# Sigmoid attention and an MLP-mixer block on one core: work by single batch in place of batch pairs, with every engine's order from a list scheduler

## The chip, the core and the metric

The kernel runs on one core of a Trainium2 chip (trn2). The metric is the device time of one execution in microseconds (us), as the median of several runs. Lower is better. Before the change it was 425.11 us, the median of three runs (424.64 to 426.28).

The engines are called as the profile calls them. PE is the TensorE (matmuls; PEld is its loading of weights), DVE the VectorE, ACT the ScalarE, POOL the GpSimd and SP the SyncE, which only issues DMA here. "PEclk" is the clock that the TensorE was granted. A profile covers one execution, and its "span" is about 1.9 us shorter than the time measured for the same execution.

## The reference

The inputs are fp32: 8 batches, 12 heads, 448 rows and 64 columns per head. The attention has no softmax. Each head's score goes through a sigmoid by itself, and the result feeds a mixer block that mixes first over rows (tokens), then over columns (channels).

```python
# cut to what matters
scores = (1/sqrt(64)) * (q @ k.T) - log(448)          # per batch and head: 448 x 448
attn   = sigmoid(scores)
x      = (attn @ v) as [8, 448, 768]                  # the 12 heads side by side

h  = relu(x.T @ w_tok1) @ w_tok2                      # 448 -> 256 -> 448, over rows
u  = x + h.T
h2 = relu(u @ w_ch1) @ w_ch2                          # 768 -> 1536 -> 768, over columns
out = u + h2
```

## The kernel before

The row number is split as `s = 7 p + j`, so a row block `j` has 64 rows. The kernel takes **two batches at a time**. Partitions 0 to 63 hold 64 rows of one batch, and partitions 64 to 127 those of the other. Six pairs of heads make up the attention of one batch pair. All matmuls are fp16.

```python
def load(g, i, what):              # g: batch pair, i: head pair
    ...                            # v: cast to fp16 by the DMA, on the gpsimd queue
    t = pa.tile([128, 2, J, E], FP32, tag="raw", ...)        # k and q: loaded as fp32 (sync queue)
    ...
    eng = nc.vector if (g, i) == (0, 0) else nc.gpsimd       # and cast by an engine
    eng.tensor_copy(out=t, in_=raw.rearrange("p h j e -> p j h e"))

def turn(i):                       # k and q with the head's column on the partitions
    if g > 0:  nc.sync.dma_start_transpose(...)              # by DMA
    else:      ... nc.tensor.transpose(...)                  # the first pair: on PE

def scores(i, j):                  # 64x64 tiles of the PE array, four matmuls side by side
    for b in range(2):
        for h in range(2):
            nc.tensor.matmul(out=ps[64*b:64*b+64, h, 0:S], lhsT=kT[i][64*h:64*h+64, j, b, :],
                             rhs=qT[i][64*h:64*h+64, :, b, :], ...)
    nc.scalar.activation(out=at, in_=ps, func=SIGMOID, bias=bias_t, scale=att_scale)

def values(i):                     # 28 matmuls on 64x64 tiles
    ...
    for b in range(2):             # then two copies on ACT
        nc.scalar.activation(out=xt[:, :, b, :], in_=ps[b]..., func=COPYF)

def back(i):  ...                  # 7 PE transposes: x with rows on the partitions
# tok1, tok2, uturn: the token stage; uturn turns u back on PE (6 transposes for each j)

def ch1(cb, j0, j1):               # j0..j1 is 0..4 or 4..7: 512 or 384 columns
    for db in range(NDB):          # 6 matmuls
        nc.tensor.matmul(out=ps, lhsT=w_ch1_t[:, db, 128*cb:128*cb+128], rhs=uT[:, db, j0:j1, :], ...)
    nc.vector.tensor_scalar(...)                             # relu

def ch2(j, half):                  # 12 matmuls of 384 columns, then add and store
    ...

def weave(att, mix):               # scores of pair g+1 spread among the mixer work of pair g
    ...

with tc.manual_schedule(engines={mybir.EngineType.PE}):      # only PE's order is given
    for _, _, f in attention_atoms(0):                       # the whole attention of pair 0 first
        f()
    for g in range(NG):
        front, rest = mixer_atoms(g)
        ...                                                  # tok1, loads of pair g+1
        weave(attention_atoms(g + 1), rest)
```

The mixer of pair 0 cannot start until all the attention of two batches is done. Only PE's order is fixed by the author; the other engines' orders are left to the framework.

Of the kernel before, what the change touches and what calls it, by code (L numbers as in the profile page):

```python
# [17 lines left out]

@with_exitstack
def kernel(  # L20
# [12 lines left out]

    nc = tc.nc
# [7 lines left out]
    NG = B // 2  # L42
    NP = H // 2
# [3 lines left out]
    JA = 4  # L47
    att_scale = 1.0 / math.sqrt(E)
    att_bias = -math.log(S)

    assert (B, H, S, E) == (8, 12, 448, 64) and D == 768 and TT == 256 and CC == 1536

    pc = ctx.enter_context(tc.tile_pool(name="pc", bufs=1))
    pa = ctx.enter_context(tc.tile_pool(name="pa", bufs=2))
    pp = ctx.enter_context(tc.tile_pool(name="pp", bufs=2, space=bass.MemoryType.PSUM))

    ident = pc.tile([128, 128], FP16, name="ident")
    bias_t = pc.tile([128, 1], FP32, name="att_bias")
    w_tok1_t = pc.tile([128, J, TT], FP16, name="w_tok1_t")
    w_tok2_s = pc.tile([128, 2, S], FP16, name="w_tok2_s")  # L60
    w_tok2_n = pc.tile([128, 2, J, P], FP16, name="w_tok2_n")
    w_ch1_t = pc.tile([128, NDB, CC], FP16, name="w_ch1_t")
    w_ch2_t = pc.tile([128, NCB, D], FP16, name="w_ch2_t")

    heads = {}

    def load(g, i, what):
        src = {"q": q, "k": k, "v": v}[what]
        if what == "v":
            t = pa.tile([128, 2, J, E], FP16, tag="vf", bufs=6, name=f"v_{g}_{i}")  # L70
        else:
            t = pa.tile([128, 2, J, E], FP32, tag="raw", bufs=4, name=f"raw{what}_{g}_{i}")
        eng = nc.gpsimd if what == "v" else nc.sync
        for b in range(2):
            eng.dma_start(  # L75
                out=t[64 * b : 64 * b + 64, :, :, :],
                in_=src[2 * g + b, 2 * i : 2 * i + 2].rearrange("h (p j) e -> p h j e", j=J),
            )
        if what != "v":
            raw = t  # L80
            t = pa.tile([128, J, 2, E], FP16, tag=f"{what}f", bufs=3, name=f"{what}_{g}_{i}")
            eng = nc.vector if (g, i) == (0, 0) else nc.gpsimd
            eng.tensor_copy(out=t[:, :, :, :], in_=raw.rearrange("p h j e -> p j h e"))  # L83
        heads[(g, i, what)] = t

    def load_pair(g, i):
        for what in ("k", "q", "v"):
            load(g, i, what)

    def load_tok_weights():  # L90
        for b in range(2):
            nc.gpsimd.dma_start(
                out=w_tok1_t[64 * b : 64 * b + 64, :, :],
                in_=moe_w_tok1.rearrange("(p j) t -> p j t", j=J),
            )
        nc.gpsimd.dma_start(
            out=w_tok2_s[:, :, :], in_=moe_w_tok2.rearrange("(tc t) s -> t tc s", tc=2)
        )
        nc.vector.tensor_copy(  # L99
            out=w_tok2_n[:, :, :, :],  # L100
            in_=w_tok2_s.rearrange("t c (p j) -> t c j p", j=J),
        )

    def load_ch_weights():
        nc.gpsimd.dma_start(
            out=w_ch1_t[:, :, :], in_=moe_w_ch1.rearrange("(db d) c -> d db c", db=NDB)
        )
        nc.gpsimd.dma_start(
            out=w_ch2_t[:, :, :], in_=moe_w_ch2.rearrange("(cb c) d -> c cb d", cb=NCB)
        )  # L110

    def bank(name, shape, dtype=FP32):
        return pp.tile(shape, dtype, tag="m", bufs=4, name=name)

    x_nats = {}

    def attention_atoms(g):

        qT, kT, attn, xT = {}, {}, {}, {}
        x_nat = pa.tile([128, J, D], FP16, tag="x_nat", bufs=2, name=f"x_nat_{g}")  # L120
        x_nats[g] = x_nat

        def turn(i):
            for what, turned in (("k", kT), ("q", qT)):
                t = pa.tile(
                    [128, J, 2, P], FP16, tag=f"{what}T", bufs=3, name=f"{what}T_{g}_{i}"
                )
                turned[i] = t
                src = heads[(g, i, what)]
                if g > 0:  # L130
                    nc.sync.dma_start_transpose(
                        out=t.rearrange("e j b p -> e j (b p)"),
                        in_=src.rearrange("p j h e -> p (j h e)"),
                    )
                    continue
                ps = bank(f"t{what}_{g}_{i}", [128, J, 2, P], FP16)
                for j in range(J):
                    nc.tensor.transpose(  # L138
                        out=ps[:, j, :, :], in_=src[:, j, :, :], identity=ident[:, :]
                    )  # L140
                nc.vector.tensor_copy(out=t[:, :, :, :], in_=ps[:, :, :, :])

        def scores(i, j):
            ps = pp.tile([128, 2, 512], FP32, tag="qk", bufs=2, name=f"qk_{g}_{i}_{j}")
            at = pa.tile([128, 2, S], FP16, tag="attn", bufs=11, name=f"attn_{g}_{i}_{j}")
            attn[(i, j)] = at
            for b in range(2):
                for h in range(2):
                    nc.tensor.matmul(  # L149
                        out=ps[64 * b : 64 * b + 64, h, 0:S],  # L150
                        lhsT=kT[i][64 * h : 64 * h + 64, j, b, :],
                        rhs=qT[i][64 * h : 64 * h + 64, :, b, :],
                        start=True,
                        stop=True,
                    )
            nc.scalar.activation(  # L156
                out=at[:, :, :],
                in_=ps[:, :, 0:S],
                func=SIGMOID,
                bias=bias_t[:, :],  # L160
                scale=att_scale,
            )

        def values(i):
            ps = [bank(f"xa_{g}_{i}_{b}", [128, S]) for b in range(2)]
            vf = heads[(g, i, "v")]
            for j in range(J):
                for h in range(2):
                    for b in range(2):
                        nc.tensor.matmul(  # L170
                            out=ps[b][64 * h : 64 * h + 64, :],
                            lhsT=vf[64 * b : 64 * b + 64, h, j, :],
                            rhs=attn[(i, j)][64 * b : 64 * b + 64, h, :],
                            start=(j == 0),
                            stop=(j == J - 1),
                        )
            xt = pa.tile([128, J, 2, P], FP16, tag="xT", bufs=2, name=f"xT_{g}_{i}")
            xT[i] = xt
            for b in range(2):
                nc.scalar.activation(  # L180
                    out=xt[:, :, b, :],
                    in_=ps[b].rearrange("d (j p) -> d j p", j=J),
                    func=COPYF,
                )

        def back(i):
            ps = bank(f"xb_{g}_{i}", [128, J, 128], FP16)
            for j in range(J):
                nc.tensor.transpose(  # L189
                    out=ps[:, j, :], in_=xT[i][:, j, :, :], identity=ident[:, :]  # L190
                )
            nc.vector.tensor_copy(  # L192
                out=x_nat[:, :, 128 * i : 128 * i + 128], in_=ps[:, :, :]
            )

        atoms = []
        nv = NP * J // 2
        for n in range(nv):

            def visit(n=n):  # L200
                for r in (2 * n, 2 * n + 1):
                    scores(r // J, r % J)

            atoms.append((float(n), 0.45, visit))
        for i in range(NP):
            atoms.append((i * J / 2 - 1.4, 0.8, lambda i=i: turn(i)))
            last = (i * J + J - 1) // 2
            atoms.append((last + 1.01, 1.4, lambda i=i: values(i)))
            atoms.append((last + 1.9, 0.4, lambda i=i: back(i)))
        return sorted(atoms, key=lambda a: a[0])  # L210

    def mixer_atoms(g):
        x_nat = x_nats[g]
        h1T = pa.tile([128, 2, 2, D], FP16, tag="h1T", bufs=1, name=f"h1T_{g}")
        uT = pa.tile([128, NDB, J, 128], FP16, tag="uT", bufs=1, name=f"uT_{g}")
        h2aT = pa.tile([128, NCB, J, 128], FP16, tag="h2aT", bufs=1, name=f"h2aT_{g}")
        us, u16s = {}, {}

        def tok1(tcb, half):
            ps = [bank(f"k1_{g}_{tcb}_{half}_{b}", [128, DH]) for b in range(2)]  # L220
            c = slice(DH * half, DH * half + DH)
            for j in range(J):
                for b in range(2):
                    nc.tensor.matmul(  # L224
                        out=ps[b][:, :],
# [168 lines left out]
```

## Time and profile before

| | before |
|---|---|
| time, median of 3 | 425.11 us |
| span of the profiled run | 421.8 us |
| PE busy / ACT busy / DVE busy | 91% / 51% / 37% |
| all matmul streaming, worked out | 341.5 us |
| first matmul of the first channel layer starts at | 85.3 us |

"Streaming" is my estimate of what the matmuls need if they never wait: all columns at 2.4 GHz plus 2.5 ns for each matmul, divided where several small tiles run side by side. The rate fits what the trace shows: twelve matmuls of 384 columns took 1.95 us and six of 512 columns 1.29 us. So 80 us of the span is not streaming. The question is where they lie.

This is from the page of the kernel before: the span, the busy times, and then rows of digits. Each row cuts the span into 40 slices of 10.5 us. A digit is the busy share of one slice in tenths; PEclk is the granted clock and DMA the mean busy share of the DMA engines.

```profile
span 421.8 us, 8216 instructions
...
PE 385.5 (91%) x3460; PEld 202.9 (48%) x3460; DVE 155.7 (37%) x276; ACT 216.9 (51%) x277; POOL 74.4 (18%) x105
...
PE   1675687899999999999999999999999999999995
...
ACT  1778866576655644675656643766565724300000
...
PEclk9999957999999999999999999999999999999999
DMA  8999999998886987027586973022202321000233
```

For eight slices PE is not full, and its clock falls to 5 tenths once. In most of these slices ACT is at 6 to 8 tenths, also not full, and DMA is nearly full. Afterwards PE is at 9 until the last slice. The loss is in front. (The granted clock of this trace is at half from 51.3 to 68.4 us, though PE never idles for more than 1.1 us there. What that can have cost is bounded further below.)

The chain of waits (start, duration, engine and output; each step is what released the one after it) tells how the front part is strung together. This is the kernel before, 0 to 90 us:

```profile
2.87 6.01 DMA rawq_0_76<-in_q_dram
...
12.40 1.01 ACT attn_0_0_184 L156
...
41.00 0.98 ACT xT_2_525 L180 x2
42.02 0.56 PE xb_2_528 L189 x7
42.58 0.34 PE qk_3_3_537 L149 x4
...
85.26 1.40 PE c_0_0_0_1160 L269 x6
```

The chain begins with a load of q. The first sigmoid is at 12.40 us. Later it runs through work like that at 41 us: ACT copies the values of head pair 2 (`xT`), PE transposes them (`xb`), and only then PE does the next scores. The same three links, read from the timeline of ACT in the kernel before (start, duration, engine, instruction; in brackets the idle time before it and who ended it):

```profile
39.98 1.01 ACT L156 ACTIVATE attn_3_2_489<-qk_3_2_488,att_bias 128x896 f16<-128x896 f32 x1
40.98 0.54 ACT L180 ACTIVATE xT_2_525<-xa_2_0_495 128x448 f16<-128x448 f32 x1
41.43 0.54 ACT L180 ACTIVATE xT_2_525<-xa_2_1_496 128x448 f16<-128x448 f32 x1
43.01 1.01 ACT L156 ACTIVATE attn_3_3_538<-qk_3_3_537,att_bias 128x896 f16<-128x896 f32 x1 [1.05 <-PE qk_3_3_537 L149]
```

Between two sigmoids of head pair 3 stand two copies, and then ACT idles 1.05 us because the scores that it needs had to wait on PE behind the transposes of those copies. The ACT copies delay PE, PE delays ACT, and neither is busy. Forty-two sigmoids of 1.01 us and their copies take from 12.4 to 66.8 us. Then the token stage follows, and the first channel matmul starts at 85.26 us.

In the same stretch DMA is loaded heavily. The DMA queues of the kernel before from 20 to 62 us (packets, MB written, share of the 16 engines; q0 is the casting queue, which writes fp16 and so reads twice what it writes):

```profile
q0 software_dynamic: 3228, 5.29, 68.0%
q1 hardware_dynamic: 3261, 5.19, 43.3%
```

So 2 x 5.29 + 5.19 = 15.8 MB were read in 42 us, or 375 GB/s.

In the steady state the loss is small and of another kind. The timeline of PE in the kernel before near 179 us:

```profile
178.99 1.46 PE L269 MATMUL c_1_1_0_2455<-uT_2117,w_ch_t 128*128 128x512 f16 x6
180.38 0.38 PE L149 MATMUL qk_0_4_2463<-qT_0_2272,kT_0_2270 64*64 64x448 f16 x4
...
180.89 0.51 PE L259 MATMUL ut_5_2481<-ident,u_1_5_2400 128*128 128x128 f16 x6
```

Each jump between full-array matmuls ("128\*128") and quarter-array ones ("64\*64") costs a little. Taken over the whole trace after 85.3 us, the time beyond streaming is 24.3 us for 159 changes of tiling, those to and from half arrays included. The Trainium skill says why: on its page "TensorEngine Tiling (Array Packing)", section "Key Properties", a change of tiling mode drains the TensorE. It gives no figure.

### The profile page before, as it was taken

The page shows a single profiled execution, that of the slowest core. Times are in us where ns is not written, and L with a number is a line of the kernel's source. Part 1 is how long each engine was busy: PE and PEld are TensorE (multiplying, and loading weights), DVE is VectorE, ACT ScalarE, POOL GpSimd, SP SyncE. Part 2 cuts the span into 40 slices and gives each one's busy share as a digit, 9 for nine tenths or more (in the row PEclk, how much of TensorE's full clock was granted, in tenths as well). Part 3 has the DMA queues.
Part 4 walks back from the last instruction along what each step waited for, and adds up shares of the span by engine and source line. Part 5 has one row for each costly group of instructions (what it writes and reads, how often), then busy time and mean ns, then how long its engine had stood idle before and what let it go on. Part 6 is the DMA issues. An engine that isn't in the chain of part 4 may idle for free.

```text
span 421.8 us, 8216 instructions
## 1 busy us (share of the span) xinstructions
PE 385.5 (91%) x3460; PEld 202.9 (48%) x3460; DVE 155.7 (37%) x276; ACT 216.9 (51%) x277; POOL 74.4 (18%) x105
## 2 busy tenths in 40 slices
PE   1675687899999999999999999999999999999995
PEld 1333344444555555544555555444555555546662
DVE  2131210843442222934432124833522225755221
ACT  1778866576655644675656643766565724300000
POOL 3852422432322122011222040000000000000000
PEclk9999957999999999999999999999999999999999
DMA  8999999998886987027586973022202321000233
GB/s 194 238 244 247 255 264 206 214 162 189 151 155 159 231 208 203 0 45 142 120 152 95 242 155 61 2 45 45 40 14 67 76 75 39 2 0 2 75 88 101
DMA packets 61429, 52.74 MB, mean 125 GB/s; under 512 B 36688, under 2 KB 56912, under 8 KB 61392
## 3 DMA queue, kind: packets, MB, share of 16 engines
q1 hardware_dynamic: 51712, 41.30, 43.2%
q0 software_dynamic: 9680, 10.92, 16.4%
q8 instruction: 27, 0.44, 0.4%
q14 instruction: 10, 0.08, 0.1%
HBM read 43.84 MB, written 11.01 MB: 130 GB/s over the span
## 4 chain that ended last, share of the span: by engine, by line
PE 84%; ACT 8%; issue 3%; DVE 2%; DMA 1%; SPq 0%; ACTq 0%; DVEq 0%
DMA rawq_0_76<-in_q_dram 1%; PE xa_0_0_273 L170 1%; PE xa_4_0_717 L170 1%; PE xa_5_0_787 L170 1%; PE c_2_6_0_4651 L288 0%; PE c_2_5_1_4602 L288 0%; PE c_2_4_1_4558 L288 0%; PE c_2_4_0_4521 L288 0%; PE c_2_3_1_4458 L288 0%; PE c_2_2_0_4382 L288 0%; PE c_2_1_1_4343 L288 0%; PE c_2_1_0_4282 L288 0%; PE c_1_5_1_3315 L288 0%; PE c_1_4_1_3271 L288 0%; PE c_1_4_0_3234 L288 0%
## 5 line engine op out<-in xcount | busy, mean ns | idle before, releaser
L269 PEld LDWEIGHTS <-w_ch_t 128*128 128x128 f16 x576 | 53.7, 98 | 54.9 <-issue 9.7
L288 PEld LDWEIGHTS <-h2aT_3405 128*128 128x128 f16 x168 | 15.6, 98 | 13.0 <-issue 3.6
L288 PEld LDWEIGHTS <-h2aT_831 128*128 128x128 f16 x168 | 15.6, 98 | 13.0 <-issue 3.6
L288 PEld LDWEIGHTS <-h2aT_2118 128*128 128x128 f16 x168 | 15.6, 98 | 13.0 <-issue 3.6
L288 PEld LDWEIGHTS <-h2aT_4692 128*128 128x128 f16 x168 | 16.4, 98 | 10.9
L242 PEld LDWEIGHTS <-w_tok_n 128*64 128x64 f16 x224 | 12.7, 108 | 9.9 <-issue 6.6
L224 PEld LDWEIGHTS <-w_tok_t 64*128 64x128 f16 x224 | 10.6, 94 | 7.8 <-issue 1.0
L138 PE MATMUL tk_0_164<-ident,k_0_74 128*128 128x128 f16 x7 | 0.9, 310 | 7.2 <-DVE k_0_74 L83 7.2
L156 ACT ACTIVATE attn_0_0_184<-qk_0_0_183,att_bias 128x896 f16<-128x896 f32 x1 | 1.0, 1007 | 10.2 <-PE qk_0_0_183 L149 10.2
L83 POOL CAST k_0_3481<-rawk_0_3478 128x896 f16<-128x896 f32 x1 | 0.9, 936 | 25.7 <-issue 25.7
L138 PEld LDWEIGHTS <-k_0_74 128*128 128x128 f16 x7 | 0.7, 139 | 7.1 <-DVE k_0_74 L83 7.1
L99 DVE COPY w_tok_n<-w_tok_s 128x896 f16<-128x896 f16 x1 | 1.6, 1575 | 5.6 <-DMA w_tok_s<-in_moe_w_tok_dram 5.6
L149 PEld LDWEIGHTS <-kT_0_163 64*64 64x64 f16 x28 | 1.1, 129 | 4.7 <-issue 4.5
L192 DVE COPY x_nat_162<-xb_4_750 128x896 f16<-128x896 f16 x1 | 0.6, 623 | 7.2 <-PE xb_4_750 L189 7.2
L149 PEld LDWEIGHTS <-kT_5_669 64*64 64x64 f16 x28 | 1.1, 131 | 4.6 <-issue 3.9
L192 DVE COPY x_nat_162<-xb_5_820 128x896 f16<-128x896 f16 x1 | 0.6, 625 | 6.8 <-PE xb_5_820 L189 6.8
L83 DVE CAST k_0_74<-rawk_0_71 128x896 f16<-128x896 f32 x1 | 1.1, 1085 | 5.1 <-DMA rawk_0_71<-in_k_dram 5.1
L83 POOL CAST k_3_3520<-rawk_3_3517 128x896 f16<-128x896 f32 x1 | 0.9, 935 | 11.5 <-DMA kT_0_3557<-k_0_3481 11.5
L75 POOL DMA_DIRECT2D v_3_953<-in_v_dram x2 | 1.2, 593 | 10.0 <-DMA w_ch_t<-in_moe_w_ch_dram 10.0
L232 ACT ACTIVATE h1T_2116<-k_1_0_0_0_2119 128x384 f16<-128x384 f32 x1 | 0.5, 491 | 4.7 <-PE k_1_0_0_1_2120 L224 4.7
L232 ACT ACTIVATE h1T_4690<-k_3_0_0_0_4693 128x384 f16<-128x384 f32 x1 | 0.5, 491 | 4.7 <-PE k_3_0_0_1_4694 L224 4.7
L232 ACT ACTIVATE h1T_3403<-k_2_0_0_0_3406 128x384 f16<-128x384 f32 x1 | 0.5, 491 | 4.7 <-PE k_2_0_0_1_3407 L224 4.7
(1538 smaller groups left out, 1079.1 us busy)
## 6 DMA issues: line engine op xcount, KB each, us to landing
w_ch_t<-in_moe_w_ch_dram POOLq DMA_DIRECT2D x2, 2304.0 KB, 30.6
rawk_0_71<-in_k_dram SPq DMA_DIRECT2D x2, 224.0 KB, 4.1
rawq_0_76<-in_q_dram SPq DMA_DIRECT2D x2, 224.0 KB, 5.7
rawk_1_89<-in_k_dram SPq DMA_DIRECT2D x2, 224.0 KB, 7.2
rawq_1_94<-in_q_dram SPq DMA_DIRECT2D x2, 224.0 KB, 7.7
rawk_2_102<-in_k_dram SPq DMA_DIRECT2D x2, 224.0 KB, 7.3
rawq_2_107<-in_q_dram SPq DMA_DIRECT2D x2, 224.0 KB, 6.3
rawk_3_119<-in_k_dram SPq DMA_DIRECT2D x2, 224.0 KB, 7.5
```

What stands on the lines that cost most here:

```text
L75: eng.dma_start(out=t[64 * b : 64 * b + 64, :, :, :], in_=src[2 * g + b, 2 * i : 2 * i + 2].rearrange("h (p j) e -> p h j e", j=J),)
L83: eng.tensor_copy(out=t[:, :, :, :], in_=raw.rearrange("p h j e -> p j h e"))
L99: nc.vector.tensor_copy(out=w_tok2_n[:, :, :, :], in_=w_tok2_s.rearrange("t c (p j) -> t c j p", j=J),)
L138: nc.tensor.transpose(out=ps[:, j, :, :], in_=src[:, j, :, :], identity=ident[:, :])
L149: nc.tensor.matmul(out=ps[64 * b : 64 * b + 64, h, 0:S], lhsT=kT[i][64 * h : 64 * h + 64, j, b, :], rhs=qT[i][64 * h : 64 * h + 64, :, b, ...
L170: nc.tensor.matmul(out=ps[b][64 * h : 64 * h + 64, :], lhsT=vf[64 * b : 64 * b + 64, h, j, :], rhs=attn[(i, j)][64 * b : 64 * b + 64, h, : ...
L192: nc.vector.tensor_copy(out=x_nat[:, :, 128 * i : 128 * i + 128], in_=ps[:, :, :])
L224: nc.tensor.matmul(out=ps[b][:, :], lhsT=w_tok1_t[64 * b : 64 * b + 64, j, 128 * tcb : 128 * tcb + 128], rhs=x_nat[64 * b : 64 * b + 64, j ...
L232: nc.scalar.activation(out=h1T[:, b, tcb, c], in_=ps[b][:, :], func=RELU)
L242: nc.tensor.matmul(out=ps[64 * b : 64 * b + 64, :], lhsT=w_tok2_n[:, tcb, j, :], rhs=h1T[:, b, tcb, c], start=(tcb == 0), stop=(tcb == 1),)
L269: nc.tensor.matmul(out=ps[:, :, :], lhsT=w_ch1_t[:, db, 128 * cb : 128 * cb + 128], rhs=uT[:, db, j0:j1, :], start=(db == 0), stop=(db == ...
L288: nc.tensor.matmul(out=ps[:, :], lhsT=h2aT[:, cb, j, :], rhs=w_ch2_t[:, cb, c], start=(cb == 0), stop=(cb == NCB - 1),)
```

## The change

The intent is to shorten the front. A single batch passes the attention before its mixer can start, so half of the sigmoids stand in front of the first channel matmul. Everything else follows from that.

- Partitions hold two heads of one batch instead of one head of two batches ("head quads": four heads at a time). Rows come in three blocks of 128 and one of 64 per batch. The 64-row tails of two batches share tiles in the last layer, so streaming does not grow there.
- k and q are cast to fp16 by the load, as v was. All loads are in one GpSimd queue in a hand-written order.
- For batches 2 to 7, a permuting DVE copy and a DMA transpose turn k and q. For batches 0 and 1 (counted from 0) PE does it. The transposes of u, too, go to DMA for batches 2 to 7.
- A list scheduler at build time (`Plan`) takes all operations with estimated durations, dependencies and buffers, and simulates the engines. **The resulting order is used for all engines.**

```diff
 # cut to its core; the rest of the kernel is rewritten in the same terms
+class Plan:
+    LAG = {"PE": 0.22, "ACT": 0.12, "DVE": 0.12, "POOL": 0.12, "LD": 0.1, "SP": 0.1}
+    ...
+    def run(self, choose):
+        lists = {}                      # one list per engine; "LD" is the loads' queue
+        ...
+        while left:
+            best = None
+            for e, ops in lists.items():
+                if e == "LD":
+                    ops = ops[:1]       # loads keep the order in which they were made
+                for o in ops:
+                    r = self.ready(o)   # operands and buffers, in estimated time
+                    if r is None:
+                        continue
+                    key = (max(r, free[e]), o.rank, r)
+                    if best is None or key < best[0]:
+                        best = (key, e, o)
+            pick = choose(self, free["PE"])
+            if pick is not None:
+                ...
+                        if kind != mode[0]:
+                            t += 0.1    # a change of PE tiling
+            ...
+            if e == "LD" or e == "SP":  # (two branches, here put together)
+                free[e] = t + o.us
+                o.end = t + o.us + 2.0  # a DMA is taken to land 2 us after its turn
+        self.log.sort(key=lambda o: o.start)
+        for o in self.log:
+            o.emit()
 ...
+    def load_qkv(b, m, what):           # one batch, one head quad
+        t = plan.buf(f"{what}f", 5 if what == "v" else 4, [128, 2, J, E], FP16, ...)
+        def emit():
+            nc.gpsimd.dma_start(out=..., in_=src[b, 4*m : 4*m+4].rearrange(...))   # casts
+        loads[(b, m, what)] = (op(f"ld_{what}_{b}_{m}", "LD", 1.45, emit, uses=[t]), t)
 ...
+        def spread():                   # w_tok2 into the order of the row blocks
+            ...
+                nc.gpsimd.tensor_copy(...)
+        c = op("spread", "POOL", 4.0, spread, after=[b], uses=[w_tok2_s, w_tok2])
 ...
+    load_all(0, 0); load_all(0, 1); load_all(0, 2)
+    tok1_ld, tok2_ld = load_w_tok()
+    load_all(1, 0); ch1_ld.append(load_ch1(0))
+    load_all(1, 1); ch1_ld.append(load_ch1(1))
+    load_all(1, 2); ch1_ld.append(load_ch1(2))
+    for i in range(3):
+        ch2_ld.append(load_ch2(i))
+    for b in range(2, B):
+        for m in range(NQ):
+            load_all(b, m)
 ...
+                if b < 2:
+                    ...                 # k and q turned on PE, copied by DVE
+                else:
+                    ...                 # permuted by DVE, then
+                        nc.sync.dma_start_transpose(...)
 ...
+            if b == 1:
+                ...                     # u turned on PE (batch 0 as well, in thirds)
+            def turn(...):              # batches 2 to 7
+                nc.sync.dma_start_transpose(out=uT[b][:, :, c0 : c0 + n], in_=u16[rows, :])
 ...
+            for i in range(0, len(rs), 2):     # score rounds in twos
+                g = rs[i : i + 2]
 ...
-    with tc.manual_schedule(engines={mybir.EngineType.PE}):
-        for _, _, f in attention_atoms(0):
-            f()
-        ...
+    with tc.manual_schedule():
+        plan.run(choose)
```

`choose` picks PE's next work: small transposes first, then score rounds when they are due, then token stage, first channel layer ("C1" below) and second ("C2").

## The prediction

> **What bounds the kernel now.** The profiled span is 421.8 us (median time 425.1). The page has PE 91% busy; the chain of waits is 84% PE. Summing all matmuls' columns at 2.4 GHz plus 2.5 ns each (twelve 128x384 matmuls took 1.95 us: that fits), half- and quarter-array ones counted as running 2 or 4 together (four 64x64 score matmuls, 0.19 to 0.22 us), I estimate 341.5 us of unavoidable PE streaming. The other 80 us:
>
> - Prologue, about 50 us. The chain puts the first channel matmul at 85.3 us, with only 34.5 us of streaming done. Until 65 us it alternates between sigmoids (42 for the first pair, about 1.0 us each) and short PE work; the slices show ACT and PE at 6 to 8 tenths, granted clock down to 0.5. DMA is saturated: from 20 to 62 us it read 15.8 MB, 375 GB/s. w_ch landed at about 67 us.
> - Steady state, about 25 us. The channel stage of pair 1 starts at 177.8, of pair 2 at 270.3: 92.5 us against 84.2 of streaming. The 8.3 us lie at the 54 changes of array tiling per pair, 0.15 us each (the timeline shows gaps of about 0.1 us around score rounds). The Trainium skill, "TensorEngine Tiling (Array Packing)", Key Properties, says that changing the mode drains the TensorE; the timeline agrees.
> - Tail, 5 us.
>
> **What the change does.** Counting the instruction streams:
>
> - PE streaming stays at 341.5 us: seven row blocks per pair become eight (tok1, tok2, transposes back: +7 us in all); six batches' transposes of u go to DMA (-7 us). Tiling changes: 195 before, 203 after.
> - k and q are cast in the load, on the GpSimd queue, where the Trainium skill, "DMA: Bandwidth & Descriptors", says a casting DMA must go; the trace does so for v and weights. POOL's 0.94 us casts go; 36 permutes come to DVE (37% busy now, about half after); 23 DMA transposes of u are added (those of k and q land in 2.9 to 3.4 us when DMA is calm).
> - A single batch passes the prologue: 21 sigmoids, not 42, before its token stage; batch 0's first channel matmuls (13.6 us) run under batch 1's sigmoids. That is the real gain.
>
> **Critical path after.** The first channel-2 matmul needs all of w_ch: 19.1 MB read before it, at 375 GB/s 51 us plus about 4 of start. It also follows 42 sigmoids and some small ACT jobs, from about 10 us on: 56 to 60. So about 60 us with 44.3 us of streaming done: 16 us lost instead of 50. Then 297.2 us of streaming, 148 tiling changes at 0.154 (22.8), tail 5, plus 3.3 between span and measured time: 388. Stalls of the fixed order: 389.
>
> **Prediction: 389 us, 380 to 401 (8 of 10).** Faster by over 2%: 0.95; within: 0.03; slower: 0.02.
>
> **What would show it.** First channel-1 matmul at about 40 us, first channel-2 at 57 to 65; later pairs still near 92 us; PE about 95% busy, ACT near 60%; matmul durations unchanged.
>
> **What would make it wrong.** One casting queue reads well below 375 GB/s (channel 2 starts late). Transposes and stores share one in-order queue: a store waiting for data, or transposes slowed by loads (up to 17 us in the old prologue), would leave PE waiting for uT or kT, some us each batch. Fixed orders on DVE and ACT could hold PSUM banks. If the scheduler hides tiling changes, it is faster than 380.

## The result and the profile after

| | before | after |
|---|---|---|
| median, same session | 425.69 us (4 runs) | 403.37 us (4 runs: 400.80, 400.98, 405.75, 407.60) |
| ratio of fast runs | 1 | 0.9464 (0.9397 to 0.953) |
| span of the profiled run | 421.8 us | 398.9 us |

A ratio here is the mean time of one kernel's fast runs over the mean of the other's fast runs of the same rounds, so it is not quite the ratio of the medians quoted. The run of 407.60 us counts as slow. The other three are fast, though they lie at two levels; the granted clock was 0.991 in the two short runs and 0.978 in that of 405.75 us.

The change is 22 us faster. The predicted direction held; the time lies 14 us above the predicted 389 us and 2.4 us above the predicted range of 380 to 401. The page of the kernel after, in the same parts as above (a slice is now 10.0 us):

```profile
span 398.9 us, 8001 instructions
...
PE 371.8 (93%) x3368; PEld 197.1 (49%) x3368; DVE 181.1 (45%) x416; ACT 213.6 (54%) x271; POOL 63.4 (16%) x95
...
PE   2898999199799999999999999999999999999995
...
ACT  1996774167655756586634758476646764220000
...
PEclk9999999799999999999999999999999999999999
DMA  7969999978934598548845798638321252031143
```

PE is nearly full from the second slice on, with two exceptions: in the eighth slice (69.8 to 79.8 us) it is busy for only one tenth and its clock drops to 7, and in the eleventh it is at 7.

From the matmuls' start times in the two traces comes this ledger. "Lost" and "excess" are the time that is not streaming.

| us | before | after |
|---|---|---|
| first C1 matmul starts | 85.3 | 42.8 |
| streaming done before it | 34.5 | 22.1 |
| **lost before it** | **50.8** | **20.7** |
| streaming after it | 307.0 | 319.3 |
| **excess after it** | **24.3** | **31.5** |
| changes of tiling after it (number) | 159 | 163 |
| tail behind the last matmul | 5.3 | 5.3 |
| span | 421.8 | 398.9 |

The front gains 30.1 us. The rest gives 7.2 us back. What was given back is seen in the waits of PE in the kernel after (total us, number of waits, longest):

```profile
PE qk L416 <- DMA qT<-qp: 8.6, 1, 8.6
PE tk L371 <- DMA k<-in_k_dram: 7.1, 3, 5.1
PE ut L682 <- ACT u_tail L669: 1.9, 1, 1.9
```

The 7.1 us for k lie before the first C1: 5.1 us at the very start, and 1.2 and 0.8 us at 32 and 41 us. The 8.6 us are one single wait. The timeline of PE around it:

```profile
66.86 2.12 PE L742 MATMUL c<-w_ch,h2aT 128*128 128x384 f16 x12
...
77.99 0.96 PE L416 MATMUL qk<-qT,kT 64*64 64x448 f16 x8 [8.55 <-DMA qT<-qp]
78.88 3.40 PE L742 MATMUL c<-w_ch,h2aT 128*128 128x384 f16 x12
...
82.86 0.57 PE L416 MATMUL qk<-qT,kT 64*64 64x448 f16 x8
...
84.02 2.11 PE L742 MATMUL c<-w_ch,h2aT 128*128 128x384 f16 x12
```

The scores of batch 2's first quad wait 8.55 us for `qT`, a DMA transpose. And what follows is slow. The eight score matmuls take 0.96 us where the next such group takes 0.57, and the twelve C2 matmuls take 3.40 us where later ones take 2.11. The Trainium skill, on the page "TensorE: Matmul & The Clock Gate", "Part 1: The HAM clock gate (the "warmup" mystery)", says that an idle window of about 3.4 us halves the clock, and that it comes back after about 3.4 us of work. The trace agrees: the granted clock is at half from 74.7 to 81.5 us, so that after 8.55 us of waiting 3.5 us of work run slow, which costs 0.39 + 1.29 = 1.7 us by these two lines (1.9 us by all matmuls concerned). Other traces show half clock after much shorter waits, of 1.85 and 2.4 us (variants 1 and 5 below), so a wait need not be as long as that window.

Why did the transpose come late? The SP queue's own timeline shows when the two were issued:

```profile
62.37 1.33 SPq L399 DMA_TRANSPOSE kT<-kp  x1
63.75 4.18 SPq L399 DMA_TRANSPOSE qT<-qp  x1
```

That of `qT` landed 14.1 us later by the chain of waits of the kernel after:

```profile
63.75 14.10 DMA qT<-qp
```

In calm stretches of the same trace such transposes land in 2.8 to 3.1 us. The DMA queues from the issue to 76.5 us explain it (columns as above):

```profile
q0 software_dynamic: 2757, 2.33, 101.2%
q1 hardware_dynamic: 1771, 0.45, 23.5%
```

The casting queue is saturated (a share above 100% comes of packets that overlap). The scheduler has let the loads of batches 2 and 3 run far ahead, and transposes of 254 bytes a packet share the engines with them. The Trainium skill, on "DMA: Bandwidth & Descriptors", section "Queues, rings and completion order", says that each DMA engine goes round-robin between its queues packet by packet. Then a queue with small packets gets little. The trace agrees in direction: 1771 packets of 254 bytes against 2757 of 845, so 0.45 MB beside 2.33 MB written. That it was this traffic which made the transposes late is tested in variant 3.

Last, the stages of the kernel after as windows (window, us, PE busy and its instructions, PEld, DVE, ACT, POOL, granted clock, DMA share, GB/s):

```profile
20.00:30.00 10.00, 9.76 (x138) 5.98 (x136) 7.14 (x17) 9.06 (x11) 9.91 (x15) 1.00 0.67 102
...
42.84:66.86 24.02, 24.02 (x232) 11.34 (x232) 11.85 (x30) 16.70 (x21) 8.00 (x12) 1.00 1.21 207
```

From 42.84 to 66.86 us PE is busy for all 24.02 us. The hole in DMA between 20 and 30 us (0.67) has its cause in the POOL timeline of the kernel after:

```profile
20.09 2.97 POOL L301 COPY w_tok<-w_tok_s 128x384 f16<-128x384 f16 x4 [4.39 <-DMA w_tok_s<-in_moe_w_tok_dram]
23.00 0.70 POOL L306 COPY w_tok<-w_tok_s 128x128 f16<-128x128 f16 x2
23.65 0.72 POOL L265 DMA_DIRECT2D v<-in_v_dram  x1
```

POOL stands 4.39 us until w_tok2 has landed, then copies for 3.6 us, and only then issues the next load. POOL's copies and the loads' issues are one in-order stream. The scheduler had modelled "POOL" and "LD" as two engines.

### The profile page after: what moved, and what is told of

The parts are those of the page before. It is cut to its first block, busy times and chain, and to the rows that moved or that the text cites. A ratio compares the mean times of both kernels' runs of the same rounds, so it can differ in the third digit from the quotient of the medians.

```text
span 398.9 us, 8001 instructions
## 1 busy us (share of the span) xinstructions
PE 371.8 (93%) x3368; PEld 197.1 (49%) x3368; DVE 181.1 (45%) x416; ACT 213.6 (54%) x271; POOL 63.4 (16%) x95
## 4 chain that ended last, share of the span: by engine, by line
PE 84%; DMA 10%; POOL 3%; issue 1%; ACT 1%; DVE 0%; POOLq 0%; ACTq 0%
PE c L710 28%; PE c L742 24%; PE qk L416 9%; PE xa L447 7%; PE yn L647 5%; PE k L549 5%; PE c L751 4%; DMA qT<-qp 4%; DMA k<-in_k_dram 3%; PE xb L485 2%; DMA w_tok_s<-in_moe_w_tok_dram 2%; DMA v<-in_v_dram 2%; POOL k L265 1%; POOL w_tok L301 1%; POOL q L265 1%
## 5 line engine op out<-in xcount | busy, mean ns | idle before, releaser
L431 ACT ACTIVATE attn<-qk,att_bias 128x896 f16<-128x896 f32 x168 | 161.5, 1007 | 94.4 <-PE qk L416 94.3
L710 PE MATMUL c<-uT,w_ch 128*128 128x448 f16 x576 | 118.8, 353 | 0.0
L742 PE MATMUL c<-w_ch,h2aT 128*128 128x384 f16 x576 | 100.7, 329 | 0.0
L722 DVE TENSOR_SCALAR h2aT<-c 128x448 f16<-128x448 f32 x96 | 59.9, 624 | 79.8 <-PE c L710 79.6
L710 PEld LDWEIGHTS <-w_ch 128*128 128x128 f16 x576 | 53.0, 98 | 55.5 <-issue 11.9
L742 PEld LDWEIGHTS <-h2aT 128*128 128x128 f16 x576 | 55.8, 99 | 40.9 <-issue 5.6
L416 PE MATMUL qk<-qT,kT 64*64 64x448 f16 x672 | 51.9, 370 | 10.9 <-DMA qT<-qp 8.6
L766 DVE TENSOR_TENSOR u<-u,c 128x384 f32<-128x384 f32 x48 | 26.6, 554 | 65.6 <-PE c L742 65.4
L265 POOL DMA_DIRECT2D v<-in_v_dram x24 | 17.2, 719 | 179.0 <-PE xa L447 164.7
L447 PE MATMUL xa<-attn,v 64*64 64x448 f16 x672 | 36.3, 350 | 0.0
L647 PE MATMUL yn<-h,w_tok 128*128 128x384 f16 x112 | 23.5, 328 | 0.0
```

The lines of the kernel that those rows point to most:

```text
L265: nc.gpsimd.dma_start(out=t.ap().rearrange("r h j e -> r h (j e)"), in_=src[b, 4 * m : 4 * m + 4].rearrange("(h s) (p j) e -> (s p) h (j e ...
L416: nc.tensor.matmul(out=ps[64 * s : 64 * s + 64, h, 0:S], lhsT=kT[64 * h : 64 * h + 64, i, s, :], rhs=qT[64 * h : 64 * h + 64, :, s, :], st ...
L431: nc.scalar.activation(out=at[:, :, :], in_=ps[:, :, 0:S], func=SIGMOID, bias=bias_t[:, :], scale=att_scale,)
L447: nc.tensor.matmul(out=ps[s][64 * h : 64 * h + 64, :], lhsT=vf[64 * s : 64 * s + 64, h, order[i], :], rhs=attn[i][64 * s : 64 * s + 64, h, :],
L647: nc.tensor.matmul(out=ps[:, :], lhsT=w_tok2[:, t, s0 : s0 + 2, :], rhs=h1[:, t, c], start=(t == 0), stop=(t == 1),)
L710: nc.tensor.matmul(out=ps[:, :], lhsT=w_ch1[cb // 4][:, db, 128 * (cb % 4) : 128 * (cb % 4) + 128], rhs=uT[b][:, db, :], start=(db == 0), ...
```

## The experiments

Two theories stood against each other. Mine: the front is short because a single batch passes it, and what came back later is a wait for DMA transposes that the saturated prefetch beside them makes late; take the traffic or the transposes away and the time falls. The rival: with every engine's order fixed, some wait will always end last; whatever is taken away at one place turns up at another, and the time stays. Further runs ask what the order of the other engines, the single batch, the changes of tiling and the transposes of u by DMA are each worth.

Differences between two variants below are differences of their ratios, times 425.7 us, so that fast runs alone are compared. The kernel after has two levels itself, of which the longer was mostly marked slow, so its ratio flatters it a little; where the medians tell more, they stand beside it. The variants ran in three sessions on three chips (control, a, c and d; b, e, f and h; i and g2), each beside the kernel before, which is one more reason to compare ratios. The scheduler makes its orders anew for every variant. "Batch" b is counted from 0.

### 1. control_after: the kernel after again, beside the others

No edit.

> The changed kernel unaltered, to see its spread. My theory: all of the miss lies before 79 us, above all in one wait of 8.6 us of PE for qT of batch 2 (the transposing DMA took 14.1 us to land) and in the half clock after it; the two levels of its times (400.9 and about 406) differ only by how long the clock stays low after waits in the first 80 us. Expected: times at 400 to 402 or at 404 to 408, span times clock near 395 in every run. Rival: the levels come from outside the kernel, and span times clock differs between them.

Measured: 404.63 us (400.14 to 406.46, six runs), ratio 0.9436 (0.9384 to 0.9488). The profiled run was slow (406.44 us). From the first C1 of batch 1 on, it agrees with the first profile to 0.01 us (288.79 us). All of the 5.7 us between the two spans lies in front of that mark. Its timeline of PE shows one more wait, longer than 3 us, with half clock behind it:

```profile
34.50 0.58 PE L371 MATMUL tk<-ident,k 128*64 128x128 f16 x14 [3.38 <-DMA k<-in_k_dram]
...
35.70 0.96 PE L371 MATMUL tq<-ident,q 128*64 128x128 f16 x14
```

Fourteen transposes of the same shape took 0.58 us before the clock fell and 0.96 us after. By the first C1 this has cost 2.9 us. Of the rest, 0.5 us is a longer wait for `qT` (9.1 us), and the granted clock shows more half clock: 10.2 us of it at that wait (6.8 us in the first profile), and another 3.4 us, from 107.1 to 110.5 us, behind the wait of 1.85 us for the tail of u. The first profile has this last wait too, but at full clock behind it. So these two executions differ by a load of k that came later and by how long the clock stays low, and not in the steady state. Span times granted clock is 392.5 to 395.7 us in the six runs, near the expected 395. Why the load came later in one of them, and why the same wait of 1.85 us is followed by half clock in one only, is not shown.

### 2. a_load20_first: the loads of batch 2's first quad earlier

```diff
+    load_all(2, 0)
     for i in range(3):
         ch2_ld.append(load_ch2(i))
     for b in range(2, B):
         for m in range(NQ):
-            load_all(b, m)
+            if (b, m) != (2, 0): load_all(b, m)
```

> k, q and v of batch 2, quad 0 are loaded before the three w_ch2 weights instead of after; the PE order is identical. Theory (queued loads delay the transposes): the transposes of batch 2 quad 0 are issued some 10 us earlier, the PE wait of 8.6 us for qT shrinks below 2 us, no half clock after it; 390 to 394 us, with a spread below 2 us. Rival (the first channel-2 matmul is then held by w_ch2, which land 3.5 us later, or the next transposes become the wait): the wait only moves; 398 to 404 us.

Measured: 401.15 us (399.62 to 403.05), ratio 0.9433 (0.9392 to 0.9474): no gain against the control in fast runs (3.5 us by the medians), though the spread is narrower. PE's order is the same. The wait for `qT` is gone; its transposes were issued at 50.66 and 52.03 us. But of the transposes of the next quad, that of `qT`, issued at 67.88 us, took 14.7 us to land. DVE's permuting copy of the fourth quad (batch 3's first) waited 4.68 us for the buffer that it was reading, and in DVE's fixed order the additions behind it waited too. PE met that in its waits:

```profile
PE yn L649 <- DVE u L768: 5.5, 1, 5.5
```

The wait had moved. Issuing one pair of transposes earlier does not help while the queue beside them is full.

### 3. c_vbufs3: hold the prefetch back

```diff
-        t = plan.buf(f"{what}f", 5 if what == "v" else 4, ...)
+        t = plan.buf(f"{what}f", 3 if what == "v" else 4, ...)
```

With three buffers for v instead of five, the one queue of loads cannot run ahead as far.

> Three buffers for v instead of five: the loads of v wait for the values matmuls, and with them, in the same queue, the prefetch of batches 2 and 3 between 60 and 80 us. Nothing else changes up to 100 us of PE order. Theory (contention with queued loads): fewer loads are in flight when the transposes of batch 2 are issued at 62 us, qT lands in under 9 us instead of 14.1, PE waits under 4 us; 394 to 399 us. Rival (the transposes are slow by themselves or by their own queue): landing stays at 12 us or more, PE wait at 7 us or more, 400 to 407 us.

Measured: 399.73 us (395.85 to 403.02), ratio 0.9319 (0.9259 to 0.9378), or 5.0 us below the control (4.9 by the medians; two of its four runs are slow). The median lies just above the expected 394 to 399. In the profiled run (slow) the transposes are issued at nearly the same time as before, 63.96 and 65.32 us. They land after 5.0 and 4.5 us, where those of the kernel after took 10.1 and 14.1 us. The DMA queues of this variant from 64 to 80 us, and then the casting queue of the kernel after from 62 to 78 us:

```profile
q1 hardware_dynamic: 5728, 1.77, 69.6%
q0 software_dynamic: 1186, 0.99, 43.1%
```

```profile
q0 software_dynamic: 3122, 2.63, 101.1%
```

PE does not wait for `qT` at all:

```profile
71.19 0.57 PE L416 MATMUL qk<-qT,kT 64*64 64x448 f16 x8
```

This is the group of scores that had waited 8.55 us; it now runs without a wait, at full clock. PE's order is that of the kernel after for the first 163 us, and the transposes are the same; what differs beside them is the traffic of the casting queue. So it was this traffic that made them late. The price comes later: loads now come too late. DVE waits 32.9 us in all for k, up to 6.0 us at once, and the part from the first C1 of batch 1 to the last matmul takes 299.1 us instead of 288.8.

### 4. d_spread_dve: the copies of w_tok2 on DVE

```diff
-                nc.gpsimd.tensor_copy(...)     # both places
+                nc.vector.tensor_copy(...)
-        c = op("spread", "POOL", 4.0, spread, ...)
+        c = op("spread", "DVE", 3.0, spread, ...)
```

> The copies that spread w_tok2 move from the GpSimd engine, where they wait for w_tok2 and hold up the loads queued behind them, to VectorE. Theory: the hole in the DMA between 20 and 24 us goes, the waits for k of batch 1 (1.2 and 0.8 us) go, the first channel-1 matmul starts at 39 to 41 us instead of 42.8; total 2 to 4 us faster: 397 to 400 us in the fast level. Rival (the hole is off the critical path, or VectorE then delays other copies): first channel-1 matmul at 42 us or later, time within 1.5 us of the control.

Measured: 397.91 us (394.52 to 399.40), ratio 0.9338 (0.9286 to 0.939): 4.2 us below the control in fast runs, 6.7 us by the medians; the two intervals just overlap. The copies cost DVE 2.0 us where POOL took 3.7, the waits for batch 1's k went, and so did the hole in DMA. The first C1, expected at 39 to 41 us, came at 42.06: that part missed, so it isn't C1's start that gains. The wait for `qT` shrank without having been touched:

```profile
PE qk L416 <- DMA qT<-qp: 5.2, 1, 5.2
```

Loads that are not held up are further along by then: the transpose of `qT` was issued at 60.73 us instead of 63.75 and took 13.0 us to land.

### 5. b_turn2_pe: batch 2's k and q turned on PE

```diff
-                if b < 2:
+                if b < 3:
```

> q and k of batch 2 are turned on the PE, as those of batches 0 and 1 are, instead of by transposing DMAs; 84 more transposes add 2.3 us of PE streaming. Theory (the transposing DMAs of batch 2 fall into the time when the loads saturate the DMA, and everything behind them waits): the PE wait for qT (8.6 to 9.1 us) and the half clock after it go, no new wait above 2 us before 100 us; 5 to 9 us faster than the control's median of 404.6: 394 to 400 us. Rival (as with the reordered loads, the wait only moves, to the next transposes or to the loads): 401 us or more.

Measured: 394.52 us (393.77 to 396.21), ratio 0.9302 (0.9263 to 0.9341): 5.7 us below the control in fast runs, 10.1 us by the medians, though it adds 2.3 us of streaming. The wait for `qT` is gone, and so is the half clock behind it. One of 2.4 us for `uT`, at 182 us, is new, and it brought 3.4 us of half clock of its own (182.1 to 185.5 us): six matmuls of 448 columns took 2.40 us there.

### 6. e_turn2_spread: both of the last two

Edit: those of 4 and 5 together.

> Both: q and k of batch 2 turned on the PE, and the spreading of w_tok2 on VectorE. Theory: the two repairs act on different stretches (20 to 43 us and 66 to 80 us) and add: 9 to 14 us below the control's median of 404.6, 390 to 396 us, near the 389 that was predicted, and a spread below 3 us. Rival (one of them already takes the other's gain): no better than the better one of them alone, 397 to 399 us.

Measured: 391.52 us (390.79 to 392.39, six runs), ratio 0.9224 (0.9195 to 0.9254). It is the best version, 9.0 us below the control in fast runs, 13.1 us by the medians. One level is left, at a granted clock of 0.999 to 1.0. From the page of this variant:

```profile
PE 373.8 (96%) x3452; PEld 199.6 (51%) x3452; DVE 182.9 (47%) x410; ACT 212.9 (54%) x271; POOL 59.9 (15%) x89
...
PE   1999999999999999998999999999999999999995
```

PE is at 96%. The ledger: first C1 at 43.0, 20.9 us lost before it, 20.8 us of excess after it (31.5 in the kernel after), span 390.6 us. So the 10.7 us that went away behind the first C1 had been waits and the half clock behind them, not a limit. In the waits of PE, no single one over 1.5 us is left once batch 0's own k has come:

```profile
PE tk L371 <- DMA k<-in_k_dram: 5.9, 1, 5.9
PE qk L416 <- ACT attn L431: 1.6, 5, 0.5
```

### 7. f_pe_only: the scheduler's order for PE alone

```diff
-    with tc.manual_schedule():
+    with tc.manual_schedule(engines={mybir.EngineType.PE}):
```

> The list scheduler's order is kept for the PE alone; the framework orders the other engines again. It moves the permutes of batch 2's k and q on VectorE ahead of evictions, to a place (about 38 us) where their loads have not landed (about 61 us). Theory that the order of every engine matters: VectorE stands still for k of batch 2, PSUM banks are not emptied, PE waits 10 us or more in the first 70 us; 412 to 430 us. Rival (the order on the PE is what counts): within 3 us of the control, 401 to 408 us.

Measured: 426.44 us (425.78 to 427.96), ratio 1.0054 (1.0013 to 1.0095): the whole gain is lost. The timelines of DVE and then of PE in this variant:

```profile
58.05 0.48 DVE L394 COPY kp<-k 128x384 f16<-128x384 f16 x2 [25.14 <-DMA k<-in_k_dram]
```

```profile
59.12 1.03 PE L485 MATMUL xb<-ident,xT 128*128 128x128 f16 x8 [25.20 <-DVE xT L472]
```

DVE took a permuting copy for batch 2 before its work for the first batches. It waited 25.14 us for the load, and the copies of the values, which PE needs for its transposes, stood behind it. The first C1 came at 68.45 us. This one wait is 25 of the 26.9 us by which the span is longer than that of the kernel after. So the single batch and PE's order are worth nothing here while the other engines' orders are left to the framework; those orders are a condition of the gain, not an addition to it.

### 8. h_single_rounds: more changes of tiling

```diff
-            for i in range(0, len(rs), 2):
-                g = rs[i : i + 2]
+            for i in range(len(rs)):
+                g = rs[i : i + 1]
```

(The place of the value matmuls is adapted.) The same work in 72 more changes of tiling.

> Score rounds are inserted one at a time from batch 1 on, not in pairs: 72 more changes of array tiling (276 against 204), the same matmuls. Theory (0.154 us for each change of tiling, as in the steady state of the kernel before): 11 us slower than the control, 412 to 418 us, PE streaming between 80 us and the end longer by about 10 us. Rival (the gaps at score rounds come from something else, such as the wait for a PSUM bank or for ACT): less than 4 us slower.

Measured: 406.34 us (405.89 to 407.83), ratio 0.9587 (0.9543 to 0.9631), 6.4 us above the control in fast runs. It lay between the two expectations. In the undisturbed part behind the first C1 of batch 1, the time beyond streaming rose from 15.24 to 22.67 us as the changes rose from 131 to 190: 7.43 / 59 = 0.126 us each. One wait of 0.56 us for u, at 190.6 us, is in this; without it 6.87 / 59 = 0.116 us each are left. In the kernel after it is 15.24 / 131 = 0.116 us each.

### 9. i_pair_prologue: two batches before the first mixer

On top of variant 6: batch 0's token stage waits for the whole attention of batch 1, which brings the pair back but leaves the scheduler.

```diff
+            wait = [o for o in visits[1] if o.name[0] == "V"] if b == 0 else []
-                o = op(f"K1_{b}_{n}_{t}", "PE", 4 * mm(w), tok1, [*need, tok1_ld, zero_op], ...)
+                o = op(f"K1_{b}_{n}_{t}", "PE", 4 * mm(w), tok1, [*need, *wait, tok1_ld, zero_op], ...)
```

> On top of the repaired kernel (batch 2 turned on the PE, spreading on VectorE; 391.5 us, first channel-1 matmul at 43.0 us with 22.1 us of PE streaming done, so 20.9 us lost): the token stage of batch 0 has to wait for the attention of batch 1, so that 42 sigmoids come before it, as in the kernel before. 37.9 us of streaming then come before the first channel-1 matmul. Theory of the prediction (passing the prologue with one batch is the real gain, 30 us): the loss before the first channel-1 matmul rises from 20.9 to 40 us or more, that matmul starts at 78 us or later, 411 us or more in all. Rival (most of the gain in the prologue comes from the order: score rounds no longer wait behind values, copies and transposes, and the first copies out of PSUM go to VectorE, so that ACT does sigmoids without gaps): the first channel-1 matmul starts at 62 to 68 us, the loss is 25 to 30 us, 396 to 402 us in all.

Measured: 403.91 us (403.68 to 405.58), ratio 0.9508 (0.9462 to 0.9553), 12.1 us above variant 6. The first C1 came at 74.67 us with 36.8 us lost before it. Both expectations missed; the value lies between them. PE now waits 9.3 us in all for sigmoids (19 waits), against 1.6 us in variant 6, and its clock is at half for 10.2 us before the first C1. The loads keep the order that was made for single batches, so a pair with an order of its own might lose less.

### 10. g2_uturn_pe: u of batches 2 to 7 turned on PE again

On top of variant 6.

```diff
-            if b == 1 and blk == 3:
-                u16 = u16_tail1
+            if blk == 3:
+                u16 = u16_tail1 if side else u16_tail0
-            if b == 1:
+            if b >= 1:
-                    a = 64 if n == 64 else 0
+                    a = 64 if n == 64 and side else 0
```

> On top of the repaired kernel (391.5 us): u of batches 2 to 7 is turned on the PE, too, instead of by 24 transposing DMAs; PE streaming rises from 343.8 to 351.8 us, tiling changes from 204 to 211. Theory (PE bound after the prologue, so moved transposes count in full): 8 to 10 us slower, 399 to 402 us. Rival (the DMA transposes hold the PE up as much as they spare it): within 3 us of 391.5.

Measured: 398.66 us (398.43 to 399.13), ratio 0.9378 (0.9329 to 0.9428), 6.6 us above variant 6 (7.1 by the medians). It adds 8.0 us of streaming (351.8 against 343.8) and 7 changes of tiling and takes away the waits for `uT`. That is a little less than the expected 8 to 10 us. So with PE at 96%, most of the time that the DMA transposes spare PE shows in the result.

| variant | median us | ratio of fast runs |
|---|---|---|
| after (control) | 404.63 | 0.9436 |
| a_load20_first | 401.15 | 0.9433 |
| c_vbufs3 | 399.73 | 0.9319 |
| d_spread_dve | 397.91 | 0.9338 |
| b_turn2_pe | 394.52 | 0.9302 |
| **e_turn2_spread** | **391.52** | **0.9224** |
| f_pe_only | 426.44 | 1.0054 |
| h_single_rounds | 406.34 | 0.9587 |
| i_pair_prologue (on e) | 403.91 | 0.9508 |
| g2_uturn_pe (on e) | 398.66 | 0.9378 |

## Why the prediction was right in kind and wrong in size

**What held.** Streaming is 341.4 us; 341.5 were predicted. The first C1 was to start at about 40 us and started at 42.8. The tail was the predicted 5 us. Later pairs were to take near 92 us: from batch 2's first C1 to batch 4's it is 91.0 us, from batch 4's to batch 6's 92.4. ACT was to be near 60% busy and was 54; DVE "about half", and was 45; PE "about 95%", and was 93. k and q were cast in the load from the GpSimd queue. The Trainium skill says on "DMA: Bandwidth & Descriptors", "SWDGE vs HWDGE vs iDMA", that only there can a DMA cast, and in both traces the casting queue is the one issued by POOL. In the kernel after, nothing in the steady state shows PE at a wait of note: behind 78.9 us there is the one of 1.9 us for the tail of u.

**What failed.** Two steps failed. The bound on the first C2 matmul left out PE's own chain (66.9 us in place of 60), and the DMA transposes were taken to cost PE nothing beside the loads (8.6 us of wait and 1.9 us of half clock). A third, the cost of a change of tiling, was mis-sized the other way and by luck hid part of this. The predicted sum was 60 + 297.2 + 22.8 + 5 = 385 us of span. Set against the trace, term by term:

| term | predicted | measured | difference |
|---|---|---|---|
| first C2 matmul starts at | 60 | 66.9 | +6.9 |
| streaming after it | 297.2 | 297.1 | -0.1 |
| changes of tiling | 148 x 0.154 = 22.8 | 147 x 0.117 = 17.2 | -5.6 |
| wait for `qT` of batch 2 | 0 | 8.6 | +8.6 |
| half clock behind it | 0 | 1.9 | +1.9 |
| wait for the tail of u | 0 | 1.9 | +1.9 |
| tail | 5 | 5.3 | +0.3 |
| span | 385.0 | 398.9 (trace: 398.9) | +13.9 |

The row of the changes of tiling is in effect what the other rows leave over; that its rate agrees with variant 8 is the check on it.

To compare with the time: the prediction had added 3.3 us from span to time and 1 us for stalls. The real offset is 1.9 us, and the median of two levels lies 2.6 us above the profiled run: 398.9 + 1.9 + 2.6 = 403.4 us (403.37 measured).

- *"The first channel-2 matmul needs all of w_ch ... It also follows 42 sigmoids ...: 56 to 60."* I took the later of the DMA bound and the ACT bound and left out the third: PE's own chain. From 42.84 to 66.86 us PE was busy for all 24.02 us, 22.2 us of it streaming and the rest 16 changes of tiling. The last part of w_ch had landed at 57.9 us, so neither DMA nor ACT set that time. Of the 6.9 us, 2.8 are the later start of the first C1. PE's work between the two marks, added to the predicted 40 us, would have given 64 beforehand.
- *"transposes slowed by loads (up to 17 us in the old prologue), would leave PE waiting for uT or kT"* was named as a risk but entered the sum with 0. It came true once, for q rather than u or k, with 8.6 us, and brought the half clock along. The deciding evidence is that the transposes stayed where they were in variant c, with less traffic beside them, landed in 4.5 us instead of 14.1, and the wait went; with PE doing the turn in variant b it went as well. Variant a shows that it is no matter of one late issue.
- *"148 tiling changes at 0.154"* was too dear. I divided all excess of the old steady state by its changes. The kernel after and h agree on 0.116 us. The old trace, taken stretch by stretch from the matmuls' start times, has nearly the same cost, 0.120 us, at the 126 changes between full and quarter arrays. Waits longer than 0.15 us make only 1.4 us of its 24.3. But 7.0 us lie in 15 stretches of half-array matmuls of the second token layer (`yn`), 0.47 us each with their waits, which the new kernel runs on the full array. So the average was carried over to a kernel that no longer has its dearest part. The saving, 5.6 us, hid part of the other misses.
- *"A single batch passes the prologue ... That is the real gain."* This is only about half true. Before the first C1 variant i loses 36.8 us, variant e 20.9 and the kernel before 50.8. So, with everything else of e in place, 15.9 of the 29.9 us saved there go when the single batch goes, in ratios of time 0.0284 of 0.0776 (12.1 of 33.0 us). The rest is what i still has over the kernel before: the scheduler's orders, the loads that cast, the first copies on DVE instead of ACT, and a cheaper steady state. That the sigmoids no longer wait behind the chain of copies, transposes and scores seen at 41 us in the kernel before fits this, but is only argued. A rival is the half clock of the kernel before, 17.1 us of it in the front. It is bounded by two runs of that kernel beside the control with a mean granted clock of 0.996 (0.978 in the profiled run), so with almost no such stretch: they took 421.62 and 422.41 us, 4.2 and 3.4 us less than the median of 425.85. So it can account for some 4 of the 22 us. Variant f shows that the orders of the engines other than PE are needed. The share of each engine, and of the casting loads, was not separated; that split stays open.

The rival, that a wait taken away turns up elsewhere, held for variant a (the wait moved to the next quad) and in part for c (late loads). It did not hold for b, d and e. In e the ledger is nearly all front, streaming and changes of tiling: of the 20.8 us behind the first C1, 165 changes at 0.117 us make 19.3.

## What to carry to other kernels

When a prologue's next mark is bounded, list PE's own chain as a bound beside DMA's and ACT's, and give any risk that has already been seen in the old trace a number in the sum. DMA transposes that PE will soon wait for did not go well beside a saturated prefetch here: hold the prefetch, or let PE turn those few tiles, and count the half clock that can follow a wait. Before a cost per event is carried to a new kernel, look which events made the average. A scheduler must model what is one in-order stream, here POOL's copies and the issues of loads, as one resource, and its order has to be imposed on every engine that stands in the chain.

## What the Trainium skill lacked or had wrong

- "TensorEngine Tiling (Array Packing)", "Key Properties", says that a change of mode drains the TensorE but gives no cost. The runs show 0.116 us each in the kernel after, and the same for the 59 added ones in h_single_rounds once a wait of 0.56 us is taken out, nearly all of them (120 of 131 in the kernel after) between 128\*128 and 64\*64, with fp16 matmuls of 128 to 448 columns.
- "DMA: Bandwidth & Descriptors", "Where 436 GB/s comes from", says that for transfers from HBM to SBUF the limit of about 358 GB/s for each core binds. With one core running, 375 GB/s were read in the kernel before (20 to 62 us), and the casting loads of the kernel after, which wrote 3.71 MB of fp16 from 43 to 61 us, read 7.42 MB, or 412 GB/s. The measured table of the same page has such values too, and the note below it says that they were taken with the pair's other core idle and that both cores streaming get about 358 GB/s each. The sentence lacks that condition.
- The same page, "DMA Transpose (X-bar)" and "Latency and other measured facts", has a rate for transposes but no landing time under load. The runs show 2.8 to 3.1 us when DMA is calm, and 14.1 and 14.7 us beside saturating casting loads, 4.5 and 5.0 us where these were held back (c_vbufs3).
- "TensorE: Matmul & The Clock Gate", "Part 1", does not give the share of busy time below which the clock is halved. The runs show half clock behind waits of 1.85 us (control_after, a_load20_first, d_spread_dve; not so in the first profile of the kernel after) and 2.4 us (b_turn2_pe), and for 17.1 us in the kernel before with no gap of PE over 1.1 us, while PE was busy for 13.3 of these 17.1 us.
